# Nine 512-token chunks, PSUM banks shared by h and attention, two native batches, and weight low parts on GpSimd in a fused linear-attention and feed-forward kernel

## The chip, the cores and the metric

The kernel runs on one core of one Trainium2 chip. The metric is the device time of one execution in microseconds (us). Before the change the median of three runs is 1052.38 us (1051.92 to 1052.93). The engines are TensorE (PE, matrix products; PEld is its weight load), VectorE (DVE), ScalarE (ACT), GpSimd (POOL) and SyncE (SP, which here only issues transfers). Each engine executes its instructions in program order and waits for data by semaphores. PSUM, into which PE writes, has eight banks of 128 partitions by 512 float32 values.

## The reference

Linear attention with random features on 8 batches of 8 heads of 576 tokens, then a feed-forward network (FFN) on the 4608 tokens:

```
q_s, k_s = q * D**-0.25, k * D**-0.25          # D = 64
phi(x) = exp(x @ omega.T - |x|^2/2 - max) / sqrt(128)   # 128 features, max over them
kv  = phi(k_s).T @ v                            # per batch and head, 128 x 64
z   = sum over tokens of phi(k_s)
out = (phi(q_s) @ kv) / (phi(q_s) @ z + 1e-6)
x   = out, heads side by side                   # 4608 x 512
h   = x @ w_in                                  # w_in 512 x 2048, float64
g   = h - tanh(h)
y   = g @ w_out                                 # w_out 2048 x 512, float64
```

The inputs q are drawn and scaled by 3.505. The weights arrive as float64 and the kernel decodes them on the chip; the result is float32 and has to be of float32 accuracy, which sets the form of all the products below.

## The kernel before, in words

**Products.** PE's fast type is `fp32r`, a float32 of fewer bits. A matrix of full accuracy is kept as two `fp32r` parts, hi and lo = x - hi, and a product is three matmuls: hi times hi, hi times lo, lo times hi. Products on plain float32 operands are called *native*; PE takes them in more passes, but nothing has to be split for them.

**FFN.** The hidden width of 2048 is cut into 16 *slices* of 128, named by one hex digit. For a chunk of tokens `ch` and a slice `s` there are five steps. `h`: 12 matmuls (4 pieces of the 512 inputs, 3 products each) into one bank, L542. `th`: ACT's tanh, L778. `g`: DVE subtracts it from h, L779, and frees the bank. `gh`: ACT rounds g to `fp32r`, L780. `gl`: DVE's rest, L781. `o`: for each 128 tokens of the chunk three matmuls of 512 columns into a `po` bank that collects over all 16 slices, L565 to L567. After slice f, `s` steps copy `po` out and SP stores it.

**Chunks.** 13 of them (`NCH`): chunk 0 has tokens 0 to 511, chunk 2 (the table's name for the next one) has 256 tokens, and the other ten have 384 (`TW`). `START` counts the native queries in units of 256 tokens, so that native query chunks 0 and 1 make FFN chunk 0.

**Attention, native.** Batches 0 to 2 take native keys (`native_k`, unit `kBC` for batch B and head pair C, 12 units): `lk` and `lv` load keys and values, `pj` projects (8 matmuls of 128 tokens and a last 64 tokens), `red` and `exp` make phi, `pk0` and `pk1` multiply it by `v` with two columns of ones beside it so that z comes along, `zt` and `zb` spread z over partitions, `kvf`, `kvwa` and `kvwd` copy kv out. The first 768 tokens take native queries (`native_q`, unit `qGP` for 256 tokens and two head pairs, 6 units): `lq`, `pj`, `red`, `exp`, `den` (DVE's denominators), `nD` and `nA` (the division by them on DVE and ACT), `pt` (transposes), `qt` (ACT's copy), `pn` (numerators), `xh` and `xl` (x and its rest).

**Attention, split.** The other 5 batches take `k_unit` (20 units) and the other 3840 tokens `q_unit` (40 units of 384 tokens and one head pair): two `fp32r` parts throughout. In a q unit L453 projects (2 matmuls of 256 columns for each 128 tokens), L606 transposes phi, L620 and L621 make the numerators; a boundary between batches in the chunk cuts those in two. In a k unit L666 makes the keys' lo and L679 the values' hi on POOL, L693 multiplies.

**Weights.** Each slice of w_in and w_out is 1 MB as float64 and goes through `decoder` (units `d0` to `df`): `is` loads it raw (ACT's queue, L994); `b`, ACT, takes the high word, scaled, as float32 (L1002); `cl` clamps it to plus and minus `TOP` (L1013, POOL; DVE for the first two slices), `engine.tensor_scalar(af, af, -TOP, TOP, op0=max, op1=min)`; `v1`, `v2`, `v3`, DVE, put the mantissa together by shifts and ors (L1019, L1025, L1033); `hi`, ACT, rounds to `fp32r` (L1041); `nh`, ACT, writes -hi (L1044); `di` is a transfer on POOL's queue that adds the float32 value onto -hi in memory (L1047), which leaves lo.

**Loads and stores.** `lv` of the native keys brings 128 rows of ten times 64 floats into a tile whose groups are 66 wide, since two columns of ones stand beside each 64 (L825). q, k and v loads and the stores go on SP's queue, the weights on ACT's.

**Order.** Every engine's order of work comes from two tables of words `unit.step.slots`. `ORDER` has the native attention, the decoder and the FFN of chunk 0; then a set of buffers is closed and `LATER` has the rest, made from `f_unit`, `q_unit`, `k_unit`, `s_unit` and `x2_unit`. `issue` walks a table word by word and calls the step, which appends its instructions to the engines' queues; the last numbers choose buffers or banks. In `LATER` the matmuls of h use banks 6 and 7, `po` uses banks 1, 2 and 3, and the attention shares the other three.

Of the kernel before, what the change touches and what calls it, by code (L numbers as in the profile page):

```python
# [23 lines left out]
TC = 256
TW = 384
START = [0, TC, 2 * TC, *range(3 * TC, NT, TW)]
NCH = len(START)
# [16 lines left out]
k12.redA k12.expB.4 q11.pj.1.0 k01.exp5.1 k00.z k00.kvf k12.expA.6 k00.zt q11.redB k01.pk1 k00.zb q11.redA
q11.expB.5 k03.lv.0 q10.den0 k20.pj.5.3.4 k12.exp5.1 k01.kvf q11.expA.7 q00.lq.0 k01.z q10.nD0 k01.zt k20.redB
k02.pj.2.0.7 q10.nA0 k12.lv.1 k20.red5 k01.zb k20.redA d0.b.0 q10.den1 q10.pt0.1 k11.lk.0 k03.pk0.6 q10.qt0.0
q10.nD1 q10.nA1 k03.pk1 k02.red5 k10.lk.2 k02.redA k20.expB.3 k02.redB q10.pt1.1 k03.kvf k10.lv.0 d0.cl
k02.expA.2 k12.pk0.3 k03.z d0.v1 k03.zt q10.qt1.1 k12.pk1 k13.lk.1 k03.zb d0.v2 k20.exp5.0 k20.expA.0
k11.pj.2.1.6 k02.lv.1 k12.z q11.den1 k12.kvf k02.exp5.1 k12.kvwa k02.expB.1 k12.zt k21.lk.0 k11.redB q10.pn.4
k12.zb k11.red5 k11.expB.6 q11.nD1 q00.pj.5.7 k12.kvwd d1.is k11.redA q10.xh d0.v3 k11.expA.4 k02.pk0.0  # L50
k11.pk0.3 q11.nA1 q10.xl d0.hi q00.redB k10.pj.1.2.4 q00.redA q01.lq.0 q00.expB.2 k02.pk1 k10.redA k23.lk.2
d0.nh k10.red5 k10.redB q11.pt1.7 k11.exp5.1 k20.lv.1 k02.z k10.expA.4 k11.pk1 d0.di k02.kvf q11.qt1.0
k10.pk0.6 d2.is k11.z k11.kvwa k10.expB.1 k11.kvwd q01.pj.1.7 k10.exp5.1 d1.b.1 k11.zt q01.redB k20.pk0.2
# [1080 lines left out]
```

## Time and profile before

| | |
|---|---|
| median of 3 runs | 1052.38 us (1051.92 to 1052.93) |
| profiled execution, span | 1049.4 us |
| instructions | 17969 |
| native stage and FFN of chunk 0 | to about 177 us |
| mean ns of one h matmul of 384 columns, `h<-xa` | 338 |
| the same of 256 columns | 283 |
| POOL busy | 283.0 us |
| small packets (under 512 B) | 18240 of 40477 |

The *span* is the time from the first to the last instruction of one profiled execution; the times of the runs lie a little above it. A group's line in the profile reads: line of code, engine, operation, output tile `<-` input tiles, shapes, count, then busy time, mean ns of one, idle time of that engine just before them and what ended it. Durations of matmuls overlap, so that the distance from one start to the next is the price of one, and a sum of durations is not the time that PE needs.

### The profile page before, as it was taken

The page shows a single profiled execution, that of the slowest core. Times are in us where ns is not written, and L with a number is a line of the kernel's source. Part 1 is how long each engine was busy: PE and PEld are TensorE (multiplying, and loading weights), DVE is VectorE, ACT ScalarE, POOL GpSimd, SP SyncE. Part 2 cuts the span into 40 slices and gives each one's busy share as a digit, 9 for nine tenths or more (in the row PEclk, how much of TensorE's full clock was granted, in tenths as well). Part 3 has the DMA queues.
Part 4 walks back from the last instruction along what each step waited for, and adds up shares of the span by engine and source line. Part 5 has one row for each costly group of instructions (what it writes and reads, how often), then busy time and mean ns, then how long its engine had stood idle before and what let it go on. Part 6 is the DMA issues. An engine that isn't in the chain of part 4 may idle for free.

```text
span 1049.4 us, 17969 instructions
## 1 busy us (share of the span) xinstructions
PE 1024.6 (98%) x5884; PEld 918.0 (87%) x5884; DVE 807.0 (77%) x2754; ACT 685.8 (65%) x1724; POOL 283.0 (27%) x445
## 2 busy tenths in 40 slices
PE   9698999999999999999999999999999999999998
PEld 8577778989999899999998889889989989999997
DVE  6499877888997987887888888888788778675222
ACT  8698766866776767667666756766766656654322
POOL 0026971304411242131331432442324500000000
PEclk9899999999999999999999999999999999999999
DMA  8777962201011101101110111101100100100000
GB/s 227 204 227 224 270 151 56 78 20 52 20 38 39 50 20 60 28 20 57 31 31 29 41 38 31 53 20 39 61 20 23 57 17 9 46 8 1 31 1 31
DMA packets 40477, 64.53 MB, mean 61 GB/s; under 512 B 18240, under 2 KB 25024, under 8 KB 38336
## 3 DMA queue, kind: packets, MB, share of 16 engines
q1 hardware_dynamic: 35696, 38.18, 12.2%
q10 hardware_dynamic: 2384, 16.81, 4.4%
q0 software_dynamic: 2304, 8.39, 4.2%
q8 instruction: 47, 0.77, 0.3%
q14 instruction: 46, 0.38, 0.1%
HBM read 45.55 MB, written 9.44 MB: 52 GB/s over the span
## 4 chain that ended last, share of the span: by engine, by line
PE 73%; DVE 14%; ACT 4%; DMA 3%; issue 3%; POOL 2%; SPq 0%; DVEq 0%; POOLq 0%; ACTq 0%
PE h L542 29%; PE po L565 9%; PE po L567 9%; PE po L566 9%; PE pt L606 2%; PE pj_q L453 2%; POOL a L1013 2%; DVE zf L593 2%; PE pk L693 2%; PE k_pk L857 2%; PE pn L620 1%; PE pn L621 1%; DVE zf L779 1%; DMA v<-va 1%; PE k_pj L834 1%
## 5 line engine op out<-in xcount | busy, mean ns | idle before, releaser
L542 PE MATMUL h<-xa,w 128*128 128x384 f32 (+1 forms) x1392 | 292.4, 347 | 1.6 <-DMA w<-a 1.6
L542 PEld LDWEIGHTS h<-xa,w 128*128 128x128 f32 x1392 | 246.1, 189 | 19.3 <-DMA w<-a 2.2
L565 PE MATMUL po<-w,zr 128*128 128x512 f32 x544 | 216.8, 398 | 0.6 <-ACT zf L794 0.5
L567 PE MATMUL po<-w,zr 128*128 128x512 f32 x544 | 213.8, 393 | 1.0 <-DVE zr L557 0.8
L566 PE MATMUL po<-w,zr 128*128 128x512 f32 x544 | 213.6, 393 | 0.0
L778 ACT ACTIVATE zf<-h 128x384 f32<-128x384 f32 (+1 forms) x170 | 84.0, 494 | 134.0 <-PE h L542 131.4
L542 PE MATMUL h<-xb,w 128*128 128x384 f32 (+1 forms) x912 | 171.2, 327 | 0.0
L779 DVE TENSOR_TENSOR zf<-h,zf 128x384 f32<-128x384 f32 (+1 forms) x170 | 95.7, 563 | 93.0 <-ACT zf L778 91.2
L542 PEld LDWEIGHTS h<-xb,w 128*128 128x128 f32 x912 | 150.7, 188 | 0.3
L567 PEld LDWEIGHTS po<-w,zr 128*128 128x128 f32 x544 | 102.1, 188 | 25.2 <-DVE zr L557 2.2
L780 ACT CAST zr<-zf 128x384 fp32r<-128x384 f32 (+1 forms) x170 | 88.5, 521 | 52.0 <-DVE zf L779 50.8
L781 DVE TENSOR_TENSOR zr<-zf,zr 128x384 fp32r<-128x384 f32 (+1 forms) x170 | 103.2, 607 | 23.5 <-ACT zr L780 21.4
L565 PEld LDWEIGHTS po<-w,zr 128*128 128x128 f32 x544 | 102.3, 188 | 12.4 <-ACT zf L794 0.9
L566 PEld LDWEIGHTS po<-w,zr 128*128 128x128 f32 x544 | 102.4, 188 | 10.7
L470 ACT ACTIVATE phi_q<-phi_q,nb_q 128x128 f32<-128x128 f32 x240 | 82.0, 395 | 22.5 <-DVE nb_q L464 21.8
L666 POOL TENSOR_TENSOR khl_A<-phi_kA,khl_A 128x256 fp32r<-128x256 f32 x40 | 33.3, 833 | 208.8 <-DVE khl_A L662 181.2
L593 DVE CUSTOM_DVE_ANT_0 zf<-phi_q,zb 128x128 f32<-128x128 f32 (+1 forms) x200 | 63.1, 315 | 13.8 <-ACT phi_q L470 2.0
L1013 POOL TENSOR_SCALAR a<-a 128x1024 f32<-128x1024 f32 x14 | 56.0, 4002 | 33.7 <-ACT a L1002 32.7
L630 DVE TENSOR_TENSOR zf<-pn,zf 64x384 f32<-64x384 f32 x80 | 44.3, 554 | 26.4 <-ACT zf L626 25.4
L626 ACT COPY zf<-pn 64x384 f32<-64x384 f32 x80 | 37.9, 474 | 38.4 <-PE pn L621 37.4
L464 DVE CUSTOM_DVE_ANT_0 phi_q<-pj_q,phi_q 128x128 f32<-128x128 f32 x240 | 58.6, 285 | 5.6 <-ACT phi_q L459 5.0
L459 ACT COPY phi_q<-pj_q 128x256 f32<-128x256 f32 x120 | 42.9, 372 | 13.8 <-PE pj_q L453 12.9
(179 smaller groups left out, 1835.7 us busy)
## 6 DMA issues: line engine op xcount, KB each, us to landing
raw<-w ACTq DMA_DIRECT2D x16, 1024.0 KB, 6.0
w<-a POOLq DMA_DIRECT2D x16, 512.0 KB, 5.8
qf<-qT SPq DMA_DIRECT2D x40, 192.0 KB, 2.4
out<-zf SPq DMA_DIRECT2D x23, 256.0 KB, 2.0
kf<-kT SPq DMA_DIRECT2D x20, 288.0 KB, 2.9
v<-vt SPq DMA_DIRECT2D x20, 288.0 KB, 2.7
v<-va SPq DMA_DIRECT2D x12, 320.0 KB, 4.0
k_f<-kT SPq DMA_DIRECT2D x12, 288.0 KB, 4.4
```

What stands on the lines that cost most here:

```text
L464: nc.vector.tensor_tensor_reduce(u[kind][:, at + i], w["pj"][:, i, :M], u[kind][:, at + i], scale=-SCALE, scalar=3.0e38, op0=ALU.add, op1= ...
L470: nc.scalar.activation(u[kind][:, at + i], u[kind][:, at + i], AF.Exp, bias=w["nb"][:, i : i + 1], scale=-1.0)
L542: nc.tensor.matmul(o, w_, x, start=i == 0, stop=i == len(prods) - 1)
L565: nc.tensor.matmul(po[t], gh[:, 2 * j + t], wt[f][:, 0, DM:], start=first, stop=False)
L566: nc.tensor.matmul(po[t], gh[:, 2 * j + t], wt[f][:, 1, DM:], start=False, stop=False)
L567: nc.tensor.matmul(po[t], gl[:, 2 * j + t], wt[f][:, 0, DM:], start=False, stop=last)
L593: nc.vector.tensor_tensor_reduce(junk[r], u["ph"][r, i], kvs[b, c][1][r, h], scale=1.0, scalar=EPS, op0=ALU.mult, op1=ALU.add, accum_out=u ...
L778: th=lambda: nc.scalar.activation(g, blocks(u["p"])[:, 0:n], AF.Tanh),
L779: g=lambda: nc.vector.tensor_sub(g, blocks(u["p"])[:, 0:n], g),
L780: gh=lambda: nc.scalar.copy(gh, g),
L781: gl=lambda: nc.vector.tensor_sub(gl, g, gh.bitcast(F32)))
L1013: engine.tensor_scalar(u["af"], u["af"], -TOP, TOP, op0=ALU.max, op1=ALU.min)
```

## The change

- **Chunks.** Nine of 512 tokens (`TW = 512`, `NCH = NT // TW`), all alike. x has a `fp32r` pair of buffers in `xa` that each chunk uses in turn, and a float32 one, `xs`.
- **Native attention** for batches 0 and 1 alone: 8 key units. Native queries are `n0` to `n3`, four groups of 256 tokens, which are chunks 0 and 1: 8 units instead of 6. Split: 24 key units and 28 query units of 512 tokens.
- **Banks.** Four for `po` (512 tokens are four blocks) and four that h, projections, transposes, numerators and the rest share by the table's numbers.
- **Weights.** The 1 MB loads go on SP's queue. All 16 clamps are on POOL, with min ahead of max. `nh` and `di` are gone; `lo` is a POOL subtraction of the rounded part from the value, 128 x 1024.
- **Norms.** The native queries' division is on POOL, four instructions of 128 columns for each `nP` step (16 steps), instead of two on DVE and two on ACT.
- **Copies.** `qt1` and the native `kvf` are on DVE; `wa` and `wd` make the split parts of batch 1's kv from that copy. The lo part of x of the pieces c = 2 and 3 is on POOL.
- **Loads.** The host writes the columns of ones beside v, and the load is one run of 2640 bytes for each of 128 rows. `omega` is doubled by the host and comes in one load.
- **Stores.** Rows of 2 KB; DVE does a part of the copies out of PSUM; the last store is split over two queues.
- **One table** for the whole program. `b.ar` closes the first stage's buffers in its middle.

The core of the diff of the code:

```diff
-    nc.sync.dma_start(u["v"][:, :, 0:D], va[b, c])
+    nc.sync.dma_start(u["v"].rearrange("p a e -> p (a e)"), va[b, c])
...
-            for h in range(2):
-                ph = u["ph", h][:, 2 * i]
-                nc.vector.tensor_scalar(ph, ph, u["dn", i][:, h : h + 1], 1.0, op0=ALU.mult, op1=ALU.mult)
...
-                ph = u["ph", h][:, 2 * i + 1]
-                nc.scalar.mul(ph, ph, u["dn", i][:, 2 + h : 3 + h])
+            for t in range(2):
+                for h in range(2):
+                    ph = u["ph", h][:, 2 * i + t]
+                    nc.gpsimd.tensor_scalar(ph, ph, u["dn", i][:, 2 * t + h : 2 * t + h + 1], 1.0, op0=ALU.mult, op1=ALU.mult)
...
-            nc.scalar.dma_start(u["raw"], w[f])
+            nc.sync.dma_start(u["raw"], w[f])
...
-            engine = nc.vector if f < 2 else nc.gpsimd
-                engine.tensor_scalar(u["af"], u["af"], -TOP, TOP, op0=ALU.max, op1=ALU.min)
+            nc.gpsimd.tensor_scalar(u["af"], u["af"], TOP, -TOP, op0=ALU.min, op1=ALU.max)
...
-        def minus_hi():
-            nc.scalar.activation(wt[f][:, 1], u["af"], AF.Copy, scale=-1.0)
         def lo():
-            nc.gpsimd.dma_start(wt[f][:, 1], u["af"], accum_op=ALU.add)
+            nc.gpsimd.tensor_sub(wt[f][:, 1], u["af"], wt[f][:, 0].bitcast(F32))
...
+        def lo(c):
+            engine = nc.vector if c < 2 else nc.gpsimd
...
+                nc.scalar.dma_start(out[r : r + P, 0 : DM // 2], u[t][:, 0 : DM // 2])
+                nc.sync.dma_start(out[r : r + P, DM // 2 :], u[t][:, DM // 2 :])
```

In the tables, a stretch of the old one with decoder and chunk 0, and the stretches of the new one that hold `d1.cl`, the load `n20.lq`, its user `n20.pj`, `da.cl`, and the end of the decoder with `dc.lo` and `f0c.h0` (in the new table the FFN unit `f0c` is chunk 0, slice c, and h comes in four words, one for each 128 inputs):

```diff
-f8.th db.v2 dd.b.1 dc.nh f8.g f9.h.0 dd.cl db.v3 f8.gh f8.gl db.hi db.nh f8.o f9.th dc.di dd.v1 de.b.2 db.di
...
+k12.kvf n10.qt0.0 k10.pj.4.6.3 k12.z n10.qt1.1 d1.b.1 db.is n01.nP1 n11.den0 k12.zt k13.expA.6 n10.pn.7 n11.den1 d1.cl
...
+f00.h0.2 k10.expA.7 d1.v1 n11.nP0 n01.pn.7 d1.v2 k13.expB.2 f00.h1 d2.cl n20.lq.1 k10.red5 n11.pt0.1 d1.v3 d8.is n01.xh
...
+n21.pj.6.0 d3.v1 d1.lo k10.kvf k11.redA dd.is f00.h2 d2.hi d3.v2 f00.h3 k11.expA.0 n20.pj.1.4 k11.red5 k10.z d6.v1 d2.lo
...
+n21.redB f02.o2 f03.th w3.wd w0.wd n21.expB.3 n20.redB f02.o3 f03.g f04.h0.1 n20.expB.7 db.cl w1.wd n21.den0 f04.h1
+f04.h2 f03.gh.1 n21.den1 f04.h3 d7.hi da.cl f05.h0.0 d8.b.2 f03.gl f05.h1 db.v1 f05.h2 f04.th d7.lo db.v2 f03.o0 f03.o1
...
+f0a.g f08.o3 dd.v3 f09.o0 f0a.gh.0 f09.o1 df.v1 dd.hi f09.o2 f0a.gl df.v2 f0b.h0.0 dd.lo f0a.o0 df.v3 f0a.o1 f09.o3
+df.hi f0a.o2 f0b.h1 df.lo f0a.o3 f0b.h2 f0b.h3 f0c.h0.1 f0b.th b.ar q20.ld k20.ld k20.lv f0c.h1 f0b.g f0c.h2 f0b.gh.1
```

More of the change, by code (lines that the diff above doesn't have):

```diff
@@ L23 @@
 NF = DFF // P
[L24 to L27, printed above, removed]
+TN = 256
+TW = 512
+NCH = NT // TW
 WB = TW // P
 E = D + 2
+NN = 2
+NW = 14
 SCALE = float(D) ** -0.25
@@ L44 @@
[L44 to L53, printed above, removed]
@@ new lines, in split_hi, with split_lo, pair, p @@
+    def split_hi(x, f):
+        for h, r in enumerate(halves):
+            nc.scalar.copy(x[r, h, :], f[r])
+    def split_lo(x, f, h):
+        nc.vector.tensor_sub(x[halves[1 - h], h, :], f[halves[h]], x[halves[h], h, :].bitcast(F32))
+    def pair(u, g, lhs, at, n, make, kind="ph"):
+        v = {}
+        def p(slot):
+            v["pj"] = tile_ps(slot, [P, 2, 2 * M], f"pj_{n}_{g}")
+            for i, x in enumerate(lhs()):
+                nc.tensor.matmul(v["pj"][:, i], x, om2, start=True, stop=True)
+        def c(*slot):
+            v["m"] = m = len(lhs())
+            if at == 0:
+                u[kind] = make(*slot)
+            nc.scalar.copy(u[kind][:, at : at + m], v["pj"][:, :m, M:])
+        def t():
+            v["nb"] = small("nb", 4, f"nb_{n}_{g}", 12)
+            for i in range(v["m"]):
+                nc.vector.tensor_tensor_reduce(
+                    u[kind][:, at + i], v["pj"][:, i, :M], u[kind][:, at + i], scale=-SCALE, scalar=3.0e38,
+                    op0=ALU.add, op1=ALU.min, accum_out=v["nb"][:, i : i + 1])
+        def e():
+            for i in range(v["m"]):
+                nc.scalar.activation(u[kind][:, at + i], u[kind][:, at + i], AF.Exp, bias=v["nb"][:, i : i + 1], scale=-1.0)
+        return {"p" + g: p, "c" + g: c, "t" + g: t, "e" + g: e}
@@ L582, in sa, with sv @@
             split_hi(u["x"], u["f"])
+        def sv():
+            for h in range(2):
+                split_lo(u["x"], u["f"], h)
         def den(t):
-            if t == 0:
-                u["dn"] = sb.tile([P, 2 * WB], F32, tag="dn", name=f"dn_{n}", bufs=8)
+            if "dn" not in u:
+                u["dn"] = small("dn", 2 * WB, f"dn_{n}", 8)
             for h in range(2):
@@ L670, in parts @@
                 return [(slice(0, P), slice(0, 2), slice(t0, t0 + 2))]
-            return [(slice(D * h, D * h + D), h, t0) for h in range(2)]
+            return [(halves[h], h, t0) for h in range(2)]
         def val_hi(slot, g, t0):
@@ L1086, in issue, with barrier, ar @@
-    def issue(order, makers):
-        units = {}
-        for token in order.split():
-            name, step_, *slot = token.split(".")
+    def barrier():
+        def ar():
+            close_pool("a0")
+            close_pool("dec")
+            env["ak"] = open_pool("ak")
+        return dict(ar=ar)
+    weight_places(open_pool("w0", "left"), range(NW))
+    env["ka"] = open_pool("ka")
+    makers = dict(k=lambda b, c: (native_k if b < NN else k_unit)(b, c), q=q_unit, n=native_q, w=split_kv, d=decoder, f=f_unit,
+                  x=x_unit, s=s_unit, b=barrier)
@@ L1090, in issue @@
+    units = {}
+    with tc.manual_schedule():
+        for token in ORDER.split():
+            name, step, *slots = token.split(".")
             if name not in units:
                 units[name] = makers[name[0]](*(int(x, 16) for x in name[1:]))
-            units[name][step_](*(int(x) for x in slot))
-    with tc.manual_schedule():
-        issue(ORDER, dict(k=native_k, q=native_q, d=decoder, f=feed))
-        close_pool("a0")
-        close_pool("dec")
-        kvf.clear()
-        ak = open_pool("ak")
-        xb[0] = ak.tile([P, 6 * TW], F32R, name="xb")
-        xb[1] = ak.tile([P, DM // P, P], F32, name="o1")
-        issue(LATER, dict(k=k_unit, q=q_unit, f=f_unit, s=s_unit, x=x2_unit))
+            units[name][step](*(int(x) for x in slots))
```

1317 lines of the change are left out of this document (587 added, 730 removed).

## The prediction

> **What bounds the kernel now.** I read the page first: the span, the busy shares and the chain that ended last.
>
> ```profile
> span 1049.4 us, 17969 instructions
> ...
> PE 1024.6 (98%) x5884; PEld 918.0 (87%) x5884; DVE 807.0 (77%) x2754; ACT 685.8 (65%) x1724; POOL 283.0 (27%) x445
> ...
> PE 73%; DVE 14%; ACT 4%; DMA 3%; issue 3%; POOL 2%; SPq 0%; DVEq 0%; POOLq 0%; ACTq 0%
> ```
>
> TensorE (PE) is busy for 98% of the span and heads the chain. The median, 1052.4 us, is 3.0 above this span; I add that 3.0 at the end. The kernel has two stages. The first (native attention, decoding of the weights, FFN of chunk 0) ends with the last 512-wide h matmul, about 177 us in. Busy times by window (columns: us, busy us of PE, PEld, DVE, ACT, POOL with counts, PE clock, DMA share, GB/s):
>
> ```profile
> 0.00:40.00 40.00, 37.52 (x386) 32.79 (x386) 26.19 (x80) 35.05 (x120) 2.41 (x16) 1.00 0.82 233
> 40.00:60.00 20.00, 11.53 (x85) 9.77 (x84) 8.00 (x32) 9.07 (x28) 0.47 (x1) 0.66 0.50 119
> 60.00:177.00 117.00, 110.78 (x602) 88.21 (x601) 98.28 (x214) 91.03 (x175) 69.89 (x31) 0.99 0.74 203
> 177.00:1049.40 872.40, 864.76 (x4816) 787.27 (x4815) 674.53 (x2431) 550.64 (x1403) 210.25 (x398) 1.00 0.11 33
> ```
>
> From 177 us on PE idles 8 us in 872: only fewer or shorter matmuls help there. In the first stage it idles 17 us, and half of that is one wait:
>
> ```profile
> PE k_pk L857 <- DMA v<-va: 8.5, 1, 8.5
> ```
> ```profile
> 36.26 2.10 SPq L825 DMA_DIRECT2D v<-va  x2
> 39.76 7.89 SPq L906 DMA_DIRECT2D q_f<-qT  x1
> ```
> ```profile
> DMA packets 40477, 64.53 MB, mean 61 GB/s; under 512 B 18240, under 2 KB 25024, under 8 KB 38336
> ```
>
> Each of the 12 `va` loads writes runs of 64 floats, 256 bytes, into rows of 66: 1280 packets, 15,360 of the 18,240 small ones. SP's next issue stuck for 7.89 us behind two of them. The clock of that window is 0.66 because PE ran at half speed during the wait and some 7 us after it, which cost about 3 us more.
>
> **The change, part by part.** First PE, which sets the end. A matmul's price is the distance from its start to the next one's, because their durations overlap:
>
> ```profile
> 900.79 0.39 PE L566 MATMUL po<-w,zr 128*128 128x512 f32 x1
> 901.02 0.39 PE L567 MATMUL po<-w,zr 128*128 128x512 f32 x1
> 901.25 1.23 PE L542 MATMUL h<-xa,w 128*128 128x384 f32 x6
> 902.31 0.40 PE L453 MATMUL pj_q<-om,qx 128*128 128x256 f32 x2
> 902.55 0.39 PE L565 MATMUL po<-w,zr 128*128 128x512 f32 x1
> ```
> ```profile
> 501.35 0.49 PE L606 MATMUL pt<-zf,phi_q 128*128 128x128 f32 x3
> 501.60 0.48 PE L693 MATMUL pk<-khl_A,vhl_A 128*128 128x256 f32 x2
> ```
>
> 512 columns take 0.23 us, 384 take 1.06/6 = 0.176, 256 take 0.12, a transpose 0.083. So a column costs 0.44 ns and a matmul some 8 ns beside: wider chunks save little.
>
> *h after chunk 0.* Counts:
>
> ```profile
> L542 PE MATMUL h<-xa,w 128*128 128x384 f32 x1200 | 243.7, 338 | 0.0
> ...
> L542 PE MATMUL h<-xb,w 128*128 128x384 f32 x720 | 146.1, 339 | 0.0
> ...
> L542 PE MATMUL h<-xb,w 128*128 128x256 f32 x192 | 25.1, 283 | 0.0
> ```
>
> Before 1920 x 0.176 + 192 x 0.12 = 360.9 us; after 8 chunks x 192 x 0.23 = 353.3: **-7.6**. The `po` matmuls stay 1728 of 512.
>
> *Split queries.* A unit of 384 has 6 projections, 6 transposes and 4 numerators: 0.72 + 0.50 + 0.72 = 1.94, 40 of them 77.6. One of 512: 0.96 + 0.66 + 0.96 (two pieces each, 0.24) = 2.58, 28 of them 72.3: **-5.3**. *Split keys.* 9 projections, 10 products, 2 turns and 2 sums over `ones` are 2.69 us; four more units: **+10.8**. The second stage: 872.4 - 2.1 = 870.3.
>
> *Native units* in the first stage, by their weight loads, which pace these short matmuls:
>
> ```profile
> 12.58 0.97 PEld L834 LDWEIGHTS k_pj<-zf,k_f 64*128 64x128 f32 x16
> 13.67 0.19 PEld L836 LDWEIGHTS k_pj<-zf,k_f 64*64 64x64 f32 x4
> 14.04 0.97 PEld L857 LDWEIGHTS k_pk<-v,zf 128*128 128x128 f32 x8 [0.17 <-issue]
> ...
> 15.81 0.30 PEld L867 LDWEIGHTS k_pk<-v,k_ph 128*128 128x128 f32 x2
> 16.24 0.97 PEld L912 LDWEIGHTS q_pj<-zf,q_f 64*128 64x128 f32 x16
> 17.34 0.19 PEld L887 LDWEIGHTS k_pk<-zf,k_z 128*128 128x128 f32 x2
> ```
> ```profile
> 24.50 0.47 PEld L950 LDWEIGHTS q_pt<-zf,q_phi 128*128 128x128 f32 x4
> ...
> 29.24 0.63 PEld L961 LDWEIGHTS q_pn<-q_qt,kvf 128*64 128x64 f32 x8 [0.17 <-issue]
> ```
>
> A key unit: 0.97 + 0.19 + 2 x 0.97 + 0.30 + 0.19 = 3.6; 12 become 8: **-14.4**. A query unit: 0.97 + 2 x 0.45 + 0.63 = 2.5; 6 become 8: **+5.0**.
>
> *Loads.* The host now packs the ones beside `v`, so a load is 128 runs of 2640 bytes: the 8.5 us wait and the 3 us of half clock go, **-11.5** (bounds 0 and -17, all idle time of the stage). What is late next is on the same queue: the sixteen 1 MB weight loads move from ACT's queue to SP's, in one row with the k, v and q loads. Ahead of the native query load of chunk 2, pair 0 (`n20.lq`), the table puts ten weight loads (10.5 MB), eight k, eight v and five q (6.4): 16.9 MB, 17.1 with its own. The weights' own queue tells a rate:
>
> ```profile
> q10 hardware_dynamic: 2384, 16.81, 4.4%
> ```
>
> 16.81 MB in 4.4% of the span, 46 us, is 364 GB/s with every engine at it; the first window moved 233. So that load lands between 47 and 73 us. PE comes to it (`n20.pj`) at about 55: 28 us of matmuls stand ahead of `d1.cl`, which falls near 40 (below), and 15 more before `n20.pj`. Bounds 0 and +18; I take **+2**, near the fast end, since the small packets that slowed the window are gone.
>
> *ACT and DVE.* ACT loses 16 `nh` copies, half the norms and half the `qt` copies; DVE takes `kvf` and half of `qt` and gives up its norms and two clamps. Neither was full in 60 to 177 us (98.3 and 91.0 of 117): counted at nothing. If that cover were gone, one slice's tanh, subtract, round and subtract would show up before `o`.
>
> *POOL* is where the work goes. The prices of before:
>
> ```profile
> L1013 POOL TENSOR_SCALAR a<-a 128x1024 f32<-128x1024 f32 x14 | 56.0, 4002 | 33.7 <-ACT a L1002 32.7 <-DVE q_dn L934 1.0
> ...
> L666 POOL TENSOR_TENSOR khl_A<-phi_kA,khl_A 128x256 fp32r<-128x256 f32 x40 | 33.3, 833 | 208.8 <-DVE khl_A L662 181.2 <-DVE dn L599 10.0 <-ACT kvw L738 9.1
> L701 POOL TENSOR_TENSOR zf<-zt 128x128 f32<-128x128 f32 x40 | 23.1, 577 | 3.1
> L1047 POOL DMA_DIRECT2D w<-a x16 | 16.4, 1026 | 59.2 <-DVE k_z L872 34.3 <-ACT w L1044 25.0
> ...
> L679 POOL CAST vhl_A<-v 128x128 fp32r<-128x128 f32 x40 | 13.7, 369 | 8.5 <-DMA v<-vt 8.4
> ...
> L679 POOL CAST vhl_M<-v 64x64 fp32r<-64x64 f32 x40 | 10.8, 271 | 2.1
> ```
>
> It loses 16 DMA issues of 1.0 us and gets two more clamps, 16 subtractions of 1024 (`lo`) and 64 norms of 128 columns. A subtraction: 256 columns cost 0.83, 128 cost 0.58, so 1024 cost 2.4 (that slope) to 3.3 (in proportion); I take 2.7. A norm: 0.37 (the cast of that size) to 0.50 (an eighth of a clamp); 0.42. Its queue is in order: a `lo` that waits for ACT's rounding holds back the clamps and norms behind it, and PE's third h matmul waits for the `lo`.
>
> The clamp decides. From `d1.cl` to the end of `dc.lo` the new table gives POOL 15 clamps, 13 `lo` and 40 norms; from `d1.cl` to `f0c.h0`, the first to need `dc.lo`, it gives PE 12 slices' h, 11 slices' o and 23 us of native work: 23 x 2.76 + 23 = 87 us. ACT has 32 us of work before `d1.cl` and was busy 35 of the first 40, so the stretch starts near 40. Without the clamps POOL has 13 x 2.7 + 40 x 0.42 = 52 us. It stays under PE's 87 while a clamp costs less than 2.3 us, and each 0.1 beyond costs 1.5 us.
>
> The row says 4.0, with max before min; the changed clamp does min first, and no row shows that. Another one-input operation, the cast, costs 0.27 at 64 columns and 0.37 at 128; carried on to 1024 that is 1.7 by the slope and 3.0 in proportion. So the bounds are 1.7 and 4.0. A middle reading comes from the tables. In the old one, nine clamps (`d7` to `df`) have on average 4.1 us of matmuls between them and their own first user, as the chip has 4.0: its spacing told the price. In the new one 2.1 us stand between a clamp and POOL's next step (15 of them; from `db.cl` to `da.cl` three h steps, 9 x 0.23), and 3.0 between a `lo` and the next. That is the planner's figure, not a measurement, but the old one held. I take 2.3: no stall, **0**, with the 4.0 kept as a rival.
>
> A row and a rule about contention: under a DVE busy for over four fifths of the time the clamps took
>
> ```profile
> L1013 POOL TENSOR_SCALAR a<-a x14: 3617/4004/4570, 59.5 to 153.5; 128x1024 f32<-128x1024 f32 x14
> ```
>
> ```profile
> L1025 DVE SCALAR_TENSOR_TENSOR a<-raw,a 128x1024 uint32<-128x1024 uint32 x16 | 22.0, 1376 | 0.2
> ```
>
> so a busy DVE adds about a tenth to the mean. The spread, 0.95 us, is within one of DVE's 1.4 us merges. If every `lo` waited out one such merge, POOL's 13 before `f0c` would bring up to 13 x 1.4 = 18 us more. The Trainium skill ("SBUF — State Buffer", "SBUF: two separate sides") calls the ports that DVE and GpSimd share an exclusive lock: the loser waits for the other's whole instruction. The spread agrees in kind, the mean says that most don't collide; by that page at its full price the sum would be 1031 + 18 = 1049.
>
> **Sum.** First stage 177 - 14.4 + 5.0 - 11.5 + 2 = 158.1; second 870.3; span 1028.4, and with the 3.0 **1031 us**.
>
> **The rivals.** *POOL at the prices of before* (slower). 15 x 4.0 + 52 = 112 us against 87: PE waits 25 us before `f0c`, spread over the slices from `f01` on: 1056. At the clamps' fastest (3.6) and `lo` at 2.4 it is 15 less, 1041; with `lo` at 3.3, 1064. For it: the only row for this shape. Against it: the reversed order and the tables' spacing. It decides from a clamp of 2.3 us and ends slower than before above 3.7. *DVE and POOL shut each other out*, 13 `lo` at 1.4 more: 1031 + 18 = 1049; for it the clamps' spread, against it their mean. *The bank.* h had two banks of its own and attention three; now four hold both, beside four for `po`. An h bank is taken for 12 x 0.23 us, then tanh and subtract:
>
> ```profile
> L778 ACT ACTIVATE zf<-h 128x512 f32<-128x512 f32 x10 | 5.9, 593 | 5.1 <-PE h L542 5.0
> ```
> ```profile
> L779 DVE TENSOR_TENSOR zf<-h,zf 128x512 f32<-128x512 f32 x10 | 6.9, 690 | 3.9 <-ACT zf L778 3.8
> ```
>
> 2.76 + 0.59 + 0.69 = 4.0 of the 6.8 us that a slice has (870/128), so attention keeps 3.4 banks of four, more than its three; against this rival. If it cost 0.1 us a slice: 1031 + 13 = 1044. *It does nothing for the wait*: the loads on SP starve the native units, +18 in place of +2: 1047.
>
> **How the numbers follow.** POOL cheap enough, 1031 (own range 1018 to 1042): 0.58. POOL at old prices, 1041 to 1064: 0.25. The other three, 1044 to 1049: 0.17. A measurement here can tell 0.2%, 2.1 us: faster is below 1050.3. The first and the last are faster but for 0.03; of the POOL rival 0.07 ends faster, 0.04 within and 0.14 slower. Faster 0.79, which I lower to 0.75 for a table that may not hold on the chip, same 0.07, slower 0.18. The range of eight in ten: 1017 (half of the stage's other idle time gone too) to 1053.
>
> **What would show it.** Right: h at 0.23 a step, 1728 of them; no wait for `va` above 1 us; clamps under 2.4 us on POOL; `f0f` done near 160 us; PE idle under 10 us after it. Wrong: clamps at 3.6 or more, PE waiting for `lo` before h in most slices; or `PE n20.pj` waiting for `qT`; or a clock at half in several windows between 60 and 160 us.

## The result and the profile after

The changed kernel takes 1114.94 us (median of 4 runs, 1114.79 to 1115.32); before took 1052.64 us beside it (4 runs). The ratio is **1.0578**, 95% interval 1.0534 to 1.0621. The forecast was 1031 us with a range of 1017 to 1053: wrong in sign. The page after, its span, busy shares, packets and chain:

```profile
span 1113.5 us, 16654 instructions
...
PE 1040.6 (93%) x5272; PEld 843.5 (76%) x5272; DVE 844.7 (76%) x2641; ACT 636.4 (57%) x1522; POOL 383.8 (34%) x598
...
DMA packets 23287, 56.00 MB, mean 50 GB/s; under 512 B 2464, under 2 KB 4896, under 8 KB 21152
...
PE 40%; DVE 32%; issue 10%; ACT 8%; POOL 8%; DMA 2%; SPq 0%; DVEq 0%; POOLq 0%; ACTq 0%
```

There are fewer matmuls and small packets, as written, and yet PE's share of the chain fell from 73% to 40% while DVE's rose from 14% to 32% and POOL's from 2% to 8%. PE now waits, for DVE above all. The busy times by window, with the stages cut where chunk 1's first h begins (192 us; columns as in the prediction):

```profile
0.00:40.00 40.00, 34.27 (x348) 29.59 (x350) 30.57 (x102) 29.16 (x93) 12.75 (x32) 0.99 0.97 373
40.00:60.00 20.00, 17.59 (x142) 13.18 (x138) 19.47 (x37) 15.00 (x37) 14.54 (x15) 0.93 0.85 340
60.00:192.00 132.00, 107.88 (x494) 84.24 (x495) 114.20 (x206) 65.67 (x122) 75.12 (x60) 0.88 0.09 31
192.00:1113.50 921.50, 880.90 (x4294) 716.46 (x4292) 680.42 (x2298) 526.54 (x1272) 281.42 (x494) 1.00 0.11 33
```

The first stage should have ended at 158 us and ends at 192, **+34**; the second should have taken 870 and takes 921.6, **+51**. In the first, DVE is busy for 30.6 + 19.5 + 114.2 = 164.2 us, which is more than the 158 that I gave the whole stage. Narrower windows show where it is full:

```profile
40.00:80.00 40.00, 32.90 (x206) 25.84 (x203) 39.44 (x58) 26.73 (x58) 25.18 (x21) 0.88 0.58 229
80.00:120.00 40.00, 30.73 (x137) 23.58 (x137) 38.82 (x80) 18.70 (x32) 28.48 (x21) 0.91 0.00 1
```

78.3 of 80 us. The rows of POOL's new work, and those of DVE that run beside it:

```profile
L631 POOL TENSOR_TENSOR w<-a,w 128x1024 fp32r<-128x1024 f32 x16 | 43.1, 2703 | 21.7 <-ACT w L628 21.7
...
L619 DVE SCALAR_TENSOR_TENSOR a<-raw,a 128x1024 uint32<-128x1024 uint32 x16 | 29.1, 1817 | 0.4
...
L623 DVE SCALAR_TENSOR_TENSOR a<-raw,a 128x1024 uint32<-128x1024 uint32 x16 | 24.4, 1526 | 0.1
...
L613 POOL TENSOR_SCALAR a<-a 128x1024 f32<-128x1024 f32 x16 | 21.1, 1322 | 25.4 <-ACT a L610 23.8 <-DVE a L623 1.2
...
L616 DVE TENSOR_SCALAR a<-a 128x1024 uint32<-128x1024 uint32 x16 | 19.0, 1184 | 2.0 <-POOL a L613 2.0
```

POOL is as cheap as I took it: `lo` 2.70 us, the clamp 1.32. But the three DVE steps of the decoder, v1 (L616), v2 (L619) and v3 (L623), went from 0.81, 1.38 and 1.34 us to 1.18, 1.82 and 1.53. The groups of v1 and v3 before (v2 stands in the prediction):

```profile
L1033 DVE SCALAR_TENSOR_TENSOR a<-raw,a 128x1024 uint32<-128x1024 uint32 x16 | 21.5, 1341 | 0.3
...
L1019 DVE TENSOR_SCALAR a<-a 128x1024 uint32<-128x1024 uint32 x16 | 13.0, 812 | 6.6 <-POOL a L1013 6.5
```

What happens to them shows in the timeline of POOL and then of DVE around one `lo` (start, duration):

```profile
107.17 1.04 POOL L613 TENSOR_SCALAR a<-a 128x1024 f32<-128x1024 f32 x1
108.18 2.44 POOL L631 TENSOR_TENSOR w<-a,w 128x1024 fp32r<-128x1024 f32 x1
```
```profile
106.88 0.34 DVE L550 CUSTOM_DVE_ANT_0 zf<-n_phi,k_zb 64x128 f32<-64x128 f32 x1
...
107.27 1.09 DVE L550 CUSTOM_DVE_ANT_0 zf<-zf,k_zb 64x128 f32<-64x128 f32 x1
...
108.39 2.37 DVE L550 CUSTOM_DVE_ANT_0 zf<-zf,k_zb 64x128 f32<-64x128 f32 x1
```

Products of one line and shape take 0.34 us, then 1.09 beside the clamp, then 2.37 beside `lo`: the last two end 0.14 to 0.15 us after POOL's instruction does (108.21 and 110.62). DVE stands still until POOL is through. Not every DVE instruction does. The next two views give minimum, median and maximum in ns of a line whose one input lies in PSUM (`h`), and of one with both inputs in SBUF, of the same shape:

```profile
L900 DVE TENSOR_TENSOR zf<-h,zf x144: 671/692/696, 63.5 to 1102.3; 128x512 f32<-128x512 f32 x144
```
```profile
L902 DVE TENSOR_TENSOR zr<-zf,zr x144: 659/692/2897, 65.8 to 1104.2; 128x512 fp32r<-128x512 f32 x144
```

The first is never stretched, the second by up to 2.2 us. To measure this I call *DVE's excess* what its instructions take above the fastest tenth of the same line and shape, summed over a stage. It is 9 and 62 us in the two stages before (cut in the same way, at 180 us), 37 and 75 after.

PE's waits, first in the first stage from 60 us, then in the second (in total, times, longest):

```profile
PE po L897 <- DVE zr L902: 6.2, 3, 4.8
PE k_pk L504 <- DVE k_z L495: 5.8, 2, 2.9
PE n_pj L540 <- DVE zf L900: 5.5, 1, 5.5
PE n_pt L565 <- POOL n_phi L559: 3.7, 2, 3.4
```
```profile
PE pt_q L711 <- DVE phi_q L706: 12.7, 21, 1.4
PE pk_k L825 <- DVE c_k L821: 4.5, 6, 1.5
PE pk_k L795 <- POOL khl_k_A L768: 3.1, 7, 0.7
```

Before, the longest of the second stage was 0.6 us in total:

```profile
PE pt L606 <- DVE nb_q L464: 0.6, 2, 0.4
```

PE also ran at half clock for 34.1 us of the first stage, in six pieces (before: 17.1 in two). Each piece begins 2 to 5 us after PE fell into a wait of 2.7 us or more.

### The profile page after: what moved, and what is told of

Read it like the earlier page. It is cut to its first block, busy times and chain, and to the rows that moved or that the text cites. A ratio compares the mean times of both kernels' runs of the same rounds, so it can differ in the third digit from the quotient of the medians.

```text
span 1113.5 us, 16654 instructions
## 1 busy us (share of the span) xinstructions
PE 1040.6 (93%) x5272; PEld 843.5 (76%) x5272; DVE 844.7 (76%) x2641; ACT 636.4 (57%) x1522; POOL 383.8 (34%) x598
## 4 chain that ended last, share of the span: by engine, by line
PE 40%; DVE 32%; issue 10%; ACT 8%; POOL 8%; DMA 2%; SPq 0%; DVEq 0%; POOLq 0%; ACTq 0%
PE h L885 16%; PE po L895 6%; PE po L897 5%; PE po L896 5%; DVE zf L698 4%; DVE zf L900 2%; DVE zr L902 2%; DVE a L619 2%; PE pt_q L711 2%; DVE phi_q L706 2%; DVE phi_q L661 2%; DVE x_q L642 2%; POOL khl_k_A L768 2%; ACT phi_q L667 1%; DVE zf L550 1%
## 5 line engine op out<-in xcount | busy, mean ns | idle before, releaser
L885 PE MATMUL h<-xa,w 128*128 128x512 f32 x1728 | 459.5, 395 | 4.0 <-ACT n_phi L443 2.4
L885 PEld LDWEIGHTS h<-xa,w 128*128 128x128 f32 x1728 | 315.6, 189 | 65.6 <-ACT n_phi L443 2.8
L897 PE MATMUL po<-w,zr 128*128 128x512 f32 x576 | 228.1, 396 | 7.0 <-DVE zr L902 7.0
L895 PE MATMUL po<-w,zr 128*128 128x512 f32 x576 | 230.1, 399 | 0.1
L896 PE MATMUL po<-w,zr 128*128 128x512 f32 x576 | 227.3, 395 | 0.0
L900 DVE TENSOR_TENSOR zf<-h,zf 128x512 f32<-128x512 f32 x144 | 99.0, 688 | 94.6 <-ACT zf L899 93.3
L899 ACT ACTIVATE zf<-h 128x512 f32<-128x512 f32 x144 | 86.0, 597 | 131.9 <-PE h L885 109.1
L902 DVE TENSOR_TENSOR zr<-zf,zr 128x512 fp32r<-128x512 f32 x144 | 107.8, 749 | 56.4 <-ACT zr L889 55.7
L889 ACT CAST zr<-zf 128x512 fp32r<-128x512 f32 x144 | 89.5, 621 | 94.9 <-DVE zf L900 66.6
L768 POOL TENSOR_TENSOR khl_k_A<-phi_Ak,khl_k_A 128x256 fp32r<-128x256 f32 x48 | 40.9, 856 | 212.1 <-DVE khl_k_A L764 177.0
L698 DVE CUSTOM_DVE_ANT_0 zf<-phi_q,zb_k 128x128 f32<-128x128 f32 (+1 forms) x240 | 80.3, 335 | 14.0 <-ACT phi_q L667 0.5
L733 DVE TENSOR_TENSOR xs<-pn_q,xs 64x512 f32<-64x512 f32 x56 | 38.5, 687 | 20.6 <-ACT xs L729 20.1
L631 POOL TENSOR_TENSOR w<-a,w 128x1024 fp32r<-128x1024 f32 x16 | 43.1, 2703 | 21.7 <-ACT w L628 21.7
L711 PE MATMUL pt_q<-zf,phi_q 128*128 128x128 f32 x224 | 34.2, 279 | 15.5 <-DVE phi_q L706 12.7
```

The lines of the kernel that those rows point to most:

```text
L698: nc.vector.tensor_tensor_reduce(junk[r], u["ph"][r, i], kvs[b, c][1][r, h], scale=1.0, scalar=EPS, op0=ALU.mult, op1=ALU.add, accum_out=u ...
L768: nc.gpsimd.tensor_sub(k[:, :m, 1], u["ph" + g[0]][:, t : t + m], k[:, :m, 0].bitcast(F32))
L885: nc.tensor.matmul(u["p"], w_, x[:, c], start=(c, i) == (0, 0), stop=(c, i) == (NC - 1, 2))
L889: nc.scalar.copy(u["gh"], g)
L895: nc.tensor.matmul(po, u["gh"][:, t], whi, start=f == 0, stop=False)
L896: nc.tensor.matmul(po, u["gh"][:, t], wlo, start=False, stop=False)
```

## The experiments

Theory 1: DVE and POOL exclude each other, as above; the change gave POOL two-input work in a stage where DVE then had no time left, so DVE's excess is PE's delay. Theory 2: the new order is at fault by itself (steps close behind their data, four banks shared, half clock), and a POOL that disturbs nobody would change little. Expectations that name a replay rest on a calculation that runs the measured durations through the program's order. The median of before differs between chips (1052.3 to 1056.0), so ratios are each to before on the same chip, and lengths of stages are those of the profiled executions. Executions of the old order spread (1048.3 to 1058.7 us for b_clamp), those of the new one lie within 2.5 us for each kernel; so differences of a few us among the kernels whose names begin with b_ are given by the ratios too. All in one table; "first stage" ends where the first h after chunk 0 starts.

| kernel | ratio to before, 95% | span | first stage | rest | DVE's excess in the two |
|---|---|---|---|---|---|
| before | | 1049.4 | 180.3 | 869.1 | 9, 62 |
| after | 1.0578 [1.0534, 1.0621] | 1113.5 | 191.9 | 921.6 | 37, 75 |
| a_lodma | 1.0599 [1.0520, 1.0679] | 1117.3 | 194.8 | 922.5 | 8, 75 |
| a_lodve | 1.0481 [1.0403, 1.0560] | 1104.8 | 183.5 | 921.3 | 11, 76 |
| a_nopool2 | 1.0402 [1.0325, 1.0480] | 1096.3 | 191.6 | 904.7 | 37, 14 |
| a_tiny | 1.0007 [0.9974, 1.0039] | 1054.0 | 169.7 | 884.3 | 10, 20 |
| a_tinylo | 1.0363 [1.0316, 1.0410] | 1092.6 | 170.9 | 921.7 | 10, 74 |
| a_tiny2 | 1.0214 [1.0175, 1.0253] | 1075.8 | 191.4 | 884.4 | 37, 18 |
| a_late | 1.0545 [1.0505, 1.0585] | 1110.7 | 191.5 | 919.2 | 37, 75 |
| b_clamp | 0.9974 [0.9940, 1.0009] | 1047.1 | 178.7 | 868.4 | 6, 62 |
| b_poollo | 1.0137 [1.0084, 1.0189] | 1067.8 | 199.0 | 868.8 | 35, 61 |
| b_va | 0.9884 [0.9855, 0.9914] | 1039.8 | 171.9 | 867.9 | 7, 62 |
| b_tiny2 | 0.9885 [0.9827, 0.9944] | 1040.9 | 179.9 | 861.0 | 7, 17 |
| b_scr512 | 1.0072 [1.0037, 1.0108] | 1062.8 | 194.5 | 868.3 | 6, 62 |

**`lo` taken away from POOL (a_lodma, a_lodve).** The first brings back the accumulating transfer, the second lets DVE subtract.

```diff
-            nc.gpsimd.tensor_sub(wt[f][:, 1], u["af"], wt[f][:, 0].bitcast(F32))
+            nc.scalar.activation(wt[f][:, 1], u["af"], AF.Copy, scale=-1.0)
+            nc.gpsimd.dma_start(wt[f][:, 1], u["af"], accum_op=ALU.add)
```
```diff
-            nc.gpsimd.tensor_sub(wt[f][:, 1], u["af"], wt[f][:, 0].bitcast(F32))
+            nc.vector.tensor_sub(wt[f][:, 1], u["af"], wt[f][:, 0].bitcast(F32))
```

> The changed kernel with the weights' low part made as before: ACT writes -hi, a transfer on POOL's queue adds the value. Theory 1 (contention): in the changed kernel the first 192 us hold 37 us of DVE time beyond the fast case of each instruction, 29 of it in instructions that overlap a 2.7 us POOL subtraction of the low part, and DVE is busy 39 of every 40 us from 40 to 120. Without those subtractions the last h of chunk 0 comes about 29 us earlier, near 163 us, and the time is 1080 to 1092. Theory 2 (order): the first stage is held by where the table puts things, whatever POOL does; the end of chunk 0 moves by less than 8 us and the time stays at 1107 to 1118. Both leave the second stage as it is, about 73 us of gaps on PE.

> The changed kernel with the low part subtracted by DVE at the same places of the table. Theory 1 (contention): DVE takes 16 x 1.4 = 22 us of work and loses 29 us of waiting, so it gains 5 to 10 us: 1105 to 1110, with the first-stage DVE excess under 10 us. Theory 2 (order): DVE was behind anyway, and 22 us more of work add 15 to 22: 1130 to 1137.

a_lodve: DVE has 20.6 us more of its own work (16 at 1.29) and the stage is still 8.4 us shorter, since its excess fell by 26. That is for theory 1 (its excess, 11, is just above the 10 expected). a_lodma missed for theory 1: the excess fell to 8, but the stage didn't shorten, and the time, 1118.7 us, is near where theory 2 had it. Its waits of POOL show another price, the transfers' own queue:

```profile
POOL w L632 <- DMA w<-a: 13.8, 2, 8.4
...
POOL w L632 <- issue: 12.1, 3, 4.2
```

The change had also cut the scratch for such transfers from 2048 bytes to 512; the changed kernel issues none. **b_scr512** tests that in the old order (before, min ahead of max, `dynamic_dma_scratch_size` 2048 to 512):

> The kernel before with min first in the clamp and 512 bytes, not 2048, of descriptor scratch for POOL's transfers, as the changed kernel has. In the changed kernel with the transfers put back POOL stood 14 us waiting for the landing of its own earlier transfers, against 2.5 us in the old order with 2048. If the small scratch is what spoiled that run, POOL waits 10 us or more here too and the time is 1054 to 1070; if the new order did, the time stays at 1047 to 1051.

Against b_clamp its first stage is 15.8 us longer, and POOL waits for its own transfers, first b_clamp, then b_scr512:

```profile
POOL w L1047 <- DMA w<-a: 2.5, 1, 2.5
```
```profile
POOL w L1047 <- DMA w<-a: 12.8, 2, 7.1
```

By the ratios it is 10 us slower than b_clamp. So a_lodma most likely carried a second cost of about the size of the one it removed, and decides nothing; the changed kernel with transfers and 2048 bytes was not run.

**POOL's two-input work of the second stage on ACT (a_nopool2).** ACT copies stand in place of POOL's subtractions and sums: the keys' lo, the sums for z and half of x's lo aren't computed.

```diff
-            nc.gpsimd.tensor_sub(k[:, :m, 1], u["ph" + g[0]][:, t : t + m], k[:, :m, 0].bitcast(F32))
+            nc.scalar.copy(k[:, :m, 1], u["ph" + g[0]][:, t : t + m])
```

> The changed kernel with POOL's two-input arithmetic after the first stage (low parts of keys and of z, sums of phi, half of x's low parts) replaced by ACT copies of the same shape, so those values are not the reference's. Theory 1 (contention): the 64 us of DVE excess of the second stage go, PE's gaps there fall from 73 us to under 30, and the time is 1070 to 1085. Theory 2 (order: each attention step stands too close behind the one that feeds it): the gaps stay above 55 us and the time is 1100 to 1116. A third reading, ACT now late, would show as waits of PE for ACT.

The rest fell by 17 us, and the time, 1098.0, is between the theories. The excess went, but ACT got the work (612 us busy in that stage, 527 after), and DVE's waits for ACT grew from 194 to 238 us; PE itself waits only 2.4 us for ACT. a_tiny2 below, with nearly the same excess and ACT as it was, falls by 37.

**POOL's two-input work made tiny (a_tiny, a_tinylo, a_tiny2).** A `memset`, which reads nothing, and then 8 or 16 columns of the subtraction or sum; the other columns are left out. a_tiny does it to the weights' lo and in the second stage, a_tinylo to the weights' lo alone, a_tiny2 to the second stage alone. The edit for `lo`:

```diff
-            nc.gpsimd.tensor_sub(wt[f][:, 1], u["af"], wt[f][:, 0].bitcast(F32))
+            nc.gpsimd.memset(wt[f][:, 1].bitcast(F32), 0.0)
+            nc.gpsimd.tensor_sub(wt[f][:, 1, 0:16], u["af"][:, 0:16], wt[f][:, 0, 0:16].bitcast(F32))
```

> The changed kernel with POOL's low parts of the weights and, after the first stage, all of POOL's two-input work cut to 8 or 16 columns behind a memset of the whole tile, so nearly all of those values are left out; no work goes to another engine, and order and waits stay. Theory 1 (DVE and POOL shut each other out): a replay of the built program with a DVE instruction on SBUF waiting for the POOL instruction under way gives 60 us less, about 1055, and DVE's excess falls from 104 to under 25 us. Theory 2 (the order alone leaves PE waiting): 1100 to 1112. If clamps and norms, which stay, do it, the first stage stays at 185 us or more.

> The changed kernel, with GpSimd's lo of the weights alone cut to its first 16 columns behind a memset (the rest of lo is left out, so values are wrong; all matmuls, ACT and DVE work and the whole second stage stay). If the exclusion between DVE and GpSimd is a matter of each stage by itself, this gives back the first stage's share and nothing more: chunk 1's h starts near 169 us (the kernel with both cuts has 169.7, the changed kernel 191.9), the second stage keeps its 921 us, span 1089 to 1093. If the stages are coupled (a late first stage shortens or lengthens the second) the second stage's length moves by over 5 us.

> The changed kernel, with GpSimd's two-input work of the second stage alone cut to 8 or 16 columns behind memsets (left out: most of the keys' lo, of the sums for z and of x's lo for two pieces). Exclusion by stage: chunk 1's h starts at 191 to 192 as in the changed kernel, the second stage falls from 921 to about 884, span 1074 to 1078. If instead GpSimd's latency on the keys' path, not DVE's lost time, is what PE waits for, it comes out the same, but DVE's excess over its own fast instructions would stay; I expect it to fall from 75 to about 20 us in that stage.

All three times came as theory 1 has it (the excess of a_tiny is 30, above the 25 expected). The weights' lo is worth 21 us and nothing beyond its stage, the second stage's work 37, and both together 59.5. PE, ACT and DVE have the same work in all of them. From 40 to 160 us POOL is still busy for 67.8 us in a_tinylo (79.6 after), since the memset alone takes 0.98 us; but it seldom holds DVE. The three steps of DVE in a_tinylo:

```profile
L623 DVE SCALAR_TENSOR_TENSOR a<-raw,a 128x1024 uint32<-128x1024 uint32 x16 | 22.3, 1396 | 0.1
...
L619 DVE SCALAR_TENSOR_TENSOR a<-raw,a 128x1024 uint32<-128x1024 uint32 x16 | 20.4, 1275 | 0.4
...
L616 DVE TENSOR_SCALAR a<-a 128x1024 uint32<-128x1024 uint32 x16 | 12.2, 761 | 2.0 <-POOL a L613 2.0
```

1.82 is back to 1.28 and 1.18 to 0.76. Of the steps that start during a memset those with two inputs aren't stretched; v1, with one, is, twice. A case of each, first POOL, then DVE:

```profile
105.41 0.95 POOL L631 MEMSET w<- 128x1024 f32 x1
...
106.92 0.95 POOL L631 MEMSET w<- 128x1024 f32 x1
```
```profile
105.50 1.41 DVE L616 TENSOR_SCALAR a<-a 128x1024 uint32<-128x1024 uint32 x1 [2.01 <-POOL a L613]
106.94 1.23 DVE L619 SCALAR_TENSOR_TENSOR a<-raw,a 128x1024 uint32<-128x1024 uint32 x1
```

v1 takes 1.41 us in place of its usual 0.68, v2 its usual 1.2.

A rival has to be told from theory 1: a tiny `lo` is also done sooner, so PE may have waited for POOL itself. In the first stage it was not so: in the chain that ended last, the `lo` instructions hold 2.4 us after and 1.1 in a_tinylo, DVE's 97.5 and 68.4. a_tinylo also runs 17 us less at half clock, and up to half of that, 8.5 us, is part of the 21. In the second stage the runs don't separate the two: the excess and POOL's delay shrink together, whichever of them PE waited for. PE's weight loads wait for the keys' lo, first after (two lines), then in a_tiny2:

```profile
PEld pk_k L795 <- POOL khl_k_A L768: 8.5, 14, 1.2
...
PEld pk_k L795 <- POOL khl_k_B L768: 4.8, 9, 1.0
```
```profile
PEld pk_k L796 <- POOL khl_k_A L769: 2.0, 5, 0.5
```

PE's own waits in that stage are 29.4 us for DVE and 4.7 for POOL after, 12.4 and none in a_tiny2. So the 37 us are the price of POOL's work; most of PE's waits are for DVE, but how much of the 37 is DVE's standing still stays open.

**The parts in the old order (b_clamp, b_poollo, b_tiny2, b_va).** b_clamp is before with min ahead of max; the others have that too.

> The kernel before with only the two operations of the clamp swapped (min first). Theory A (the order of the operations sets POOL's rate): the 14 clamps on POOL fall from 4.0 to about 1.3 us, and since PE idles 6 us between 60 and 177 us, the time falls by 2 to 8 us, to 1045 to 1050. Theory B (the clamps of before were slow for another reason, such as a busy DVE): they stay at 3.5 to 4.5 us and the time at 1052.

Theory A holds for the rate; the clamp itself fell from 4.00 us to 1.45:

```profile
L1013 POOL TENSOR_SCALAR a<-a 128x1024 f32<-128x1024 f32 x14 | 20.3, 1449 | 39.7 <-ACT a L1002 39.7
```

The time is the same within its interval: POOL's clamps were covered.

```diff
-            nc.scalar.activation(wt[f][:, 1], u["af"], AF.Copy, scale=-1.0)
+            pass
-            nc.gpsimd.dma_start(wt[f][:, 1], u["af"], accum_op=ALU.add)
+            nc.gpsimd.tensor_sub(wt[f][:, 1], u["af"], wt[f][:, 0].bitcast(F32))
```

> The kernel before with min first in the clamp and, in place of the -hi copies and the accumulating transfers, the subtraction of the low part on POOL: that part of the change inside the old order. Theory 1 (DVE and POOL shut each other out): 16 subtractions of 2.7 us add about 29 us of waiting to a DVE that was busy 98 of 117 us there; by the replay the time is 20 us over the 1049 of the swapped clamp alone, 1062 to 1072. Theory 2 (the new order is the cause, the subtraction is harmless and saves a 9 us transfer): 1040 to 1050.

This is the changed subtraction alone, in an order that has nothing else of the change: 20.3 us more in the first stage and 28 more of excess, after which the rest runs as before (by the ratios 17 us in all, for theory 1). No POOL instruction stands in the first stage's part of the chain that ended last, while DVE's grow there from 29 to 68 us against b_clamp, so it is again DVE that pays. POOL is less busy here than before with its slow clamps (56 of 117 us against 70; b_clamp 35), DVE more:

```profile
60.00:177.00 117.00, 97.66 (x494) 75.76 (x495) 105.86 (x169) 64.18 (x128) 56.09 (x27) 0.91 0.36 126
```

b_tiny2 makes POOL's two-input work of the old second stage, on keys and z, tiny, by the same edits as a_tiny2 there; x's lo, which a_tiny2 also cuts, isn't POOL's in the old kernel.

> The kernel before with min first in the clamp, and POOL's two-input work on keys and z after the first stage cut to 8 or 16 columns behind a memset of the tile (those values are left out): the same cut that the changed kernel had. In the kernel before the DVE excess after 177 us is 62 us, about as much as the 75 us of the changed kernel, but PE's gaps there are 17 us against 73. Reading 1 (the exclusion costs time wherever it is, as much as DVE waits): 25 to 40 us less than the 1049 of the swapped clamp alone, 1010 to 1025. Reading 2 (the old order covers it, because its steps stand far enough apart; the new order lost that cover): 0 to 12 us less, 1037 to 1049.

Reading 2: 45 us of excess go, and the time falls by 6 to 7 us (9 by the ratios). Of 57 us that go in a_tiny2 the new kernel gets 37 back; the old one covers most of its own.

b_va takes only the packed load of the change:

```diff
-            nc.sync.dma_start(u["v"][:, :, 0:D], va[b, c])
+            nc.sync.dma_start(u["v"].rearrange("p a e -> p (a e)"), va[b, c])
```

> The kernel before with min first in the clamp and with v packed by the host with its columns of ones, one run of 2640 bytes a row, for all 12 loads. Reading 1 (my term): the 8.5 us wait for va and 3 us at half clock go, 11 us off the 1049.3 of the swapped clamp alone: 1036 to 1041. Reading 2 (the time is given back by the next late thing: decoder and DVE hold the first stage anyway): 1045 to 1050.

It is faster than both kernels, by 1.2% than before (0.9884 [0.9855, 0.9914]). The median, 1043.1 us, lies between the two readings; against b_clamp it gains 7 us in the profiled executions and 9 by the ratios. PE's wait for `va`, first b_clamp, then b_va:

```profile
PE k_pk L857 <- DMA v<-va: 7.2, 1, 7.2
```
```profile
PE k_pk L857 <- DMA v<-va: 2.2, 1, 2.2
```

The half clock of the first stage fell from 17.1 us to 10.2.

**The transposes one step later (a_late).** In the new second stage the transposes of the queries mostly start right behind the norm that they wait for: in the median the first weight load of a step starts 0.12 us after the end of its norm, 1.79 in the old order. 37 h or o steps were put ahead of the transposes in front of them, which makes 40 of the 56 steps later (the expectation says 37):

```diff
-q23.z0.1 f1d.gl q23.z1.2 q23.a0 k33.pA0.4 f1d.o0
+q23.z0.1 f1d.gl f1d.o0 q23.z1.2 q23.a0 k33.pA0.4
```

> The changed kernel, where 37 of the 56 steps of transposes of the second stage are put one PE step later: the next h or o step, whose data are ready, is put ahead of them; nothing else is moved and nothing is left out. If the order's closeness by itself costs the second stage its time (transposes right behind the norm that they wait for), each moved step hides 0.7 us more, and the wait of the transposes for DVE's norm (12.7 us) falls by more than half: span 1100 to 1107. If DVE is the full engine and PE waits for it wherever it is placed, the wait only moves to another step: span 1111 to 1117.

The waits of a_late in the second stage:

```profile
PE pt_q L793 <- DVE phi_q L788: 5.9, 11, 1.4
...
PE po L979 <- DVE zr L984: 2.0, 5, 0.5
PE pn_q L808 <- DVE ql_q L801: 1.7, 4, 0.9
PE pn_q L807 <- DVE ql_q L801: 1.7, 3, 1.0
```

The wait of the transposes halves, 12.7 to 5.9, and the stage gains 2.4 us of its 51. The rest turned up one step on, at the numerators (1.7 each) and at o (2.0, before the move 0.8). Theory 2 in this simple form falls. The span, 1110.7, is at the second reading's edge, though DVE isn't full in this stage on average (680 of 919 us).

## Why the prediction was wrong

*The step that failed* is "ACT and DVE ... Neither was full in 60 to 177 us (98.3 and 91.0 of 117): counted at nothing." DVE was 84% busy, and the forecast shortened the stage by a tenth on top: 132.5 us of DVE's work before, in a stage of 158, is the same 84%, with some 25 us free. I then held 13 `lo` of 2.7 us against POOL's queue alone. All 16 cost DVE 28 us of standing still (37 of excess in place of 9), which is more than it had free. Before, the same job was a transfer, beside which the excess was 9 (8 in a_lodma). a_tinylo and b_poollo show this cause alone: 21 and 20 us.

*The rival "DVE and POOL shut each other out"* had the right mechanism and the wrong payer. I let POOL wait for DVE's 1.4 us merges, 18 us in all, and set them against PE. The traces show the wait on DVE's side: `lo` took 2.70 us on average against 2.44 in the piece above, so POOL waited some 4 us in sixteen of them, and DVE got the excess. I also took the clamps' mean as evidence that "most don't collide"; but a clamp that isn't stretched may still stretch others: with the shorter one, in b_clamp, v1 fell from 0.81 to 0.69 us. I had read the rows from POOL's side only. The Trainium skill ("SBUF — State Buffer", "SBUF: two separate sides") says that whoever of the two starts first holds the pair for the whole instruction, and that a DVE instruction takes part if it runs in a two-port mode, or if it has two SBUF inputs and GpSimd's reads SBUF; the trace agrees (L902 stretched by up to 2.2 us, L900 with an input in PSUM never, v2 beside a memset not).

*"The second stage: 872.4 - 2.1 = 870.3"* kept PE's 8 idle us. The matmuls' arithmetic held; three h matmuls and one o step after:

```profile
533.73 0.84 PE L885 MATMUL h<-xa,w 128*128 128x512 f32 x3
534.41 0.39 PE L895 MATMUL po<-w,zr 128*128 128x512 f32 x1
534.63 0.39 PE L896 MATMUL po<-w,zr 128*128 128x512 f32 x1
```

0.68 for three and 0.22 for the next, as taken (0.23). What I missed is that a stage which is bound by PE stays so only if the order keeps steps ready ahead of it. DVE's excess was there before, 62 us of it, and hidden: where it is removed from the old order, 6 to 7 us come back, from the new one 37. This pair shows that the covering lies in the rest of the kernel, its order, banks and chunks together; which of them, and which steps of the new order would have to move, it doesn't (a_late tried one kind).

*The loads.* Half right. The `va` wait is gone after the change, none is left above 1 us; PE never waits for `qT` at `n20.pj`, so the starved loads fall as a rival. The gain of 11.5 us is not shown in full: alone, in b_va, it is 7 us (9 by the ratios), with 2.2 us of the wait and 10.2 us at half clock left.

*POOL's price.* The clamp at 1.32 us is below both my 2.3 and my lower bound of 1.7; `lo` at 2.70 as taken; a norm 0.52 against 0.42. POOL was busy 34% and was not the bound; the rival of old prices falls. Its lower end was also summed wrongly: clamps at 3.6 and `lo` at 2.4 take off 15 x 0.4 + 13 x 0.3 = 10 us and not 15, so 1046 and not 1041.

*The banks.* PE waits for a bank in one place of the list above, `n_pj` for the h that DVE hadn't yet taken (5.5 us), and that is again DVE's lateness.

*The sum.* Forecast span 1028.4. POOL's work on SBUF adds 59.5 (22 and 37, a_tiny against after), and 25.6 stay: a_tiny has 169.7 + 884.3 in place of 158.1 + 870.3. a_tiny still runs 13.7 us at half clock in the first stage, and in the second its matmuls start some 35 us in all later than the median distance of their shape, 18 of them at the transposes (17 in all before, 72 after). No run here isolates these; they stay open.

## What to carry to other kernels

Count a moved step's price on every engine that shares a path with the one that gets it: GpSimd work that reads SBUF, two inputs or one as in the clamp, is paid for by DVE, here up to its whole length, and costs little only where DVE has slack or the order keeps other work ready. Look for it in the spread of DVE's rows (minimum, median, maximum of one shape) beside GpSimd's, and add DVE's busy time over the stage as it will be, not as it was. A gain that hangs on one wait, like the packed load here, is worth trying alone before a new order for the whole program.

## What was not expected of the hardware

- The order of min and max in one GpSimd instruction: 4.00 us with max first, 1.32 to 1.45 with min first, for 128 x 1024 float32.
- A DVE instruction that GpSimd's `lo` or clamp holds ends later than that one by its own undisturbed time less 0.13 to 0.14 us: 0.14 us for the products of 0.28, 0.55 for L902 (0.68), 1.08 for v2 (1.21). GpSimd's memset of the same size (0.98 us) holds none with two inputs, but v1, which has one.
- 512 bytes in place of 2048 for the scratch of GpSimd's transfers cost 16 us with sixteen of them (10 by the ratios).
- The half clock came in pieces of 3.4 us and multiples of it (3.4, 6.8, 10.2, in the old order also 13.7 and 17.1).
